# The second products of a feed-forward layer: 576 output columns as 384 and 192 instead of 288 and 288

## The chip, the core and the metric

The kernel runs on one core of a Trainium2 chip. The metric is device time in microseconds, the median of three runs. The engines are named as in the profile: PE (TensorE, products), PEld (its weight loads), DVE (VectorE), ACT (ScalarE), POOL (GpSimd), SP (SyncE, here mostly a queue that issues DMAs).

## The reference, cut to what matters

```python
def reference(A_u, A_A_re, ..., B_x, B_w1, B_w2):
    x = A_u                                   # 1 x 2048 x 576
    xn = _layernorm(x, axis=-1)
    return x + _A_ref(xn, ...) + _B_ref(xn, B_w1, B_w2)

def _B_ref(x, w1, w2):
    h = jnp.einsum("bsd,df->bsf", x, w1)      # 576 -> 4608
    h = _silu(h)
    return jnp.einsum("bsf,fd->bsd", h, w2)   # 4608 -> 576

def _A_ref(u, A_re, A_im, B_re, B_im, C_re, C_im, log_dt, Dskip):
    ...
    P = jnp.exp(logdA[:, :, None] * l[None, None, :])
    K = jnp.einsum("dn,dnl,dn->dl", Cc, P, dB).real   # a kernel of 2048 taps per channel
    ...                                               # FFT convolution of u with K
    return y + u * Dskip
```

The input x is normalised and goes two ways: through a long convolution whose kernel K is generated from a state-space model (128 states for each of 576 channels), and through a feed-forward layer with SiLU. Both results are added to x. All of it is in float32.

## The kernel before

**The feed-forward layer.** The 2048 rows are two halves of two blocks of 512 rows; a block is four row tiles of 128 (`j` is the row tile, 0 to 15). The 4608 hidden columns are nine chunks of `FT = 4` tiles of 128. Every pair of half, chunk and block is one entry of `blocks`, 36 in all. Each float32 operand is split into a high part, rounded to the format that PE multiplies in one pass (`F32R`), and a low part, the rest; a product of two such operands is three products: high by high, high by low, low by high. So `split_w1` and `split_w2` make `h1, l1` and `h2, l2` (ACT copies the high part, DVE subtracts for the low one), and `up` makes `gh, gl`.

`up(blk, t)` is a first product: 14 products of 512 columns into an accumulator `ph`, then SiLU and the copy to `gh` on ACT (L339, L340) and the subtraction to `gl` on DVE (L342). `down(blk, jj)` is the second product of one row tile with the four hidden tiles of the chunk: for each half of the 576 output columns (`HD = 288`) one accumulator `po`, 4 tiles by three products of 288 columns (L357), and an add of `po` to the row tile's sum `acc[j]` on DVE (L361). All accumulators `po` come from `ps2`, which has three buffers. The products of `up` use `ps1`, with two; everything else uses `pss`, with three.

**The order.** For each block eight steps are issued: `u0` of the next block, `d0` to `d3` of this one, `u1`, `u2`, `u3` of the next. The loads and splits of the next chunk's weights are hung behind steps. `weave` runs these 2 x 9 x 2 x 8 = 288 steps, and after each lets the generator `side()` go on to the share of the steps that it has asked for. `side()` does in turn: the normalisation and the transposes, the preparation of the parameters, the generation of K (`kgen`, between `marks[0]` and `marks[1]`; with it `spread`, the first transform of u), the spectral products (`spectral`, between `marks[1]` and `marks[2]`), and `tail`, which adds the convolution to the row tiles at the times `tail_at`. `kgen` works mostly on DVE (L637 to L676) with small products on PE (L696, L711); `spectral` uses all three engines (L826 is its products) and ends in `yo`, written to `d2`; `add_conv` reads it back as `ys` and multiplies once more (`py`, L847).

The order within an engine's queue is not this order: a scheduler places the instructions by a model of their times, priority going by the order of issue. `tc.high_priority()` lifts instructions (the adds of `po` and the SiLU group among them), and `behind(ins)` puts instructions after a given one on its engine. On the chip every engine then works through its own fixed queue.

**The end.** Row tiles 14 and 15 are stored last; row tile 15 in two halves of 288 columns (`store`, L184), each in four DMAs by two queues. The last chunk's weights for tiles 2 and 3 go into the pool `yp`, which opens when the spectral stage's pool `kl` has closed (L269, L304).

Of the kernel before, what the change touches and what calls it, by code (L numbers as in the profile page):

```python
# [11 lines left out]
F32 = mybir.dt.float32  # L12
F32R = mybir.dt.float32r
# [6 lines left out]
P = 128  # L20
L = 2048
D = 576
# [2 lines left out]
NJ = 16  # L25
NKT = 4
HD = D // 2
NFT = FF // P
MAGIC = 12582912.0
TWO_PI = float(np.nextafter(np.float32(2 * math.pi), np.float32(0)))  # L30
# [13 lines left out]
def kernel(  # L44
# [21 lines left out]
    nc = tc.nc  # L66
    FT = 4
    NCH = NFT // FT

# [4 lines left out]
    def quarters(v, engines):  # L74

        for q in range(4):
            yield slice(32 * q, 32 * q + 32), v[q // 2, q % 2], engines[q % len(engines)]
# [28 lines left out]
    wp = ctx.enter_context(tc.tile_pool(name="wp", bufs=2))  # L106
    gp = ctx.enter_context(tc.tile_pool(name="gp", bufs=6))
    ps1 = ctx.enter_context(tc.tile_pool(name="ps1", bufs=2, space=PSUM))
    ps2 = ctx.enter_context(tc.tile_pool(name="ps2", bufs=3, space=PSUM))
    pss = ctx.enter_context(tc.tile_pool(name="pss", bufs=3, space=PSUM))  # L110

    acc = {}
# [27 lines left out]
    pins = {}  # L140

    def behind(ins):
        return tc.issue_after(ins) if ins is not None else nullcontext()

    def spread(up):
# [3 lines left out]
        for j in range(NJ):  # L149
            src = up.tile([P, D], F32, tag="xr", name="xr")  # L150
            nc.sync.dma_start(src, dxn[:, j])
            for m in range(2):
# [5 lines left out]
                for h in range(2):  # L158
                    hs = slice(h * HD, (h + 1) * HD)
                    pu = pss.tile([P, 512], F32, tag="pss", name="pu")  # L160
                    nc.tensor.matmul(pu[:, :HD], s1[:, 0, :], sp[:, hs], start=True, stop=False)  # L161
                    nc.tensor.matmul(pu[:, :HD], s1[:, 1, :], sp[:, hs], start=False, stop=True)  # L162
                    nc.scalar.copy(u1[:, hs], pu[:, :HD])
                nc.gpsimd.dma_start(
# [3 lines left out]
    def load_x(j, pool, tag, engines):  # L168

        t = pool.tile([P, 2, D], F32, tag=tag, name=f"{tag}{j}")  # L170
        for i in range(2 if j == 0 else 1):
            for ps, v, eng in quarters(xv, engines):
                if j:
                    eng.dma_start(t[ps], v[:, j:j + 2])
                else:
                    eng.dma_start(t[ps, i], v[:, i])
        pairs[j] = t
        return t[:, 0, :], t[:, 1, :]

    def store(t, j, engines):  # L180

        for hs in (slice(0, HD), slice(HD, D)) if j == NJ - 1 else (slice(0, D),):
            for ps, v, eng in quarters(ov, engines):
                eng.dma_start(v[:, j:j + 2] if len(t.shape) > 2 else v[:, j, hs], t[ps] if len(t.shape) > 2 else t[ps, hs])  # L184

    def norm(p0, js, xs):
# [4 lines left out]
        for i in range(n):  # L191
            for h in range(2):
                nc.vector.bn_stats(out=st[:, i, h, :], in_=xs[i][:, h * HD:(h + 1) * HD])
            nc.vector.bn_aggr(out=mv[:, i, :], in_=st[:, i, :, :])
# [62 lines left out]
    def ffn():  # L257
        w2v = w2.rearrange("(t p) d -> p t d", p=P)
        blocks = [(half, c, b) for half in range(2) for c in range(NCH) for b in range(2)]
        W1, W2, G = {}, {}, {}  # L260
# [47 lines left out]
        def split_w2(half, c, t):  # L308
            first = half == 0 and c == 0
            r2 = R2.pop((half, c, t))  # L310
            h2 = wp.tile([P, D], F32R, tag="w2h", name="w2h", bufs=FT + 1)
            l2 = wp.tile([P, D], F32R, tag="w2l", name="w2l", bufs=FT + 1)
            with behind(pins["xt_s"] if first else pins["gh"]):
                pins["w2h"] = nc.scalar.copy(h2, r2).ins  # L314
            with behind(pins["w1l"] if first else None):
                pins["w2l"] = nc.vector.tensor_sub(l2, r2, h2).ins
            if first and t == 0:
                pins["w2l0"] = pins["w2l"]
            W2[half, c, t] = h2, l2

        def up(blk, t, a=0, e=512, after=None):

# [21 lines left out]
        def down(blk, jj):  # L344
            half, c, b = blk
            j = 8 * half + 4 * b + jj
            js = slice(jj * P, (jj + 1) * P)
            if half == 1 and c == NCH - 1:
                if jj % 2 == 0:
                    add_conv(j, (acc[j], acc[j + 1]))  # L350
            for h in range(2):
                hs = slice(h * HD, (h + 1) * HD)
                po = ps2.tile([P, 512], F32, tag="ps2", name="po")
                n = 0
                for t in range(FT):
                    for g, w in ((0, 0), (0, 1), (1, 0)):
                        pins["pe"] = nc.tensor.matmul(po[:, :HD], G[blk, t][g][:, js], W2[half, c, t][w][:, hs],  # L357
                                                      start=n == 0, stop=n == 3 * FT - 1).ins
                        n += 1
                with tc.high_priority():  # L360
                    nc.vector.tensor_add(acc[j][:, hs], po[:, :HD], acc[j][:, hs])  # L361
            if half == 0 and c == NCH - 1:
                rows = slice(j * P, (j + 1) * P)
                nc.sync.dma_start(dr0[rows, :], acc[j])
                if j % 2:
                    acc[7 + j], acc[8 + j] = load_x(7 + j, accp, "acc", (nc.sync,))
# [42 lines left out]
        for i, blk in enumerate(blocks):  # L409
            half, c, b = blk  # L410
# [451 lines left out]

    def side():
        nonlocal s4, kl, yp, pa, tail_at
        marks = (0.13, 0.597, 0.823)
        tail_at = (0.91, 0.934, 0.967, 0.0072)
        with tc.tile_pool(name="kf", bufs=1) as kfp:
            for n in ("f", "phi"):
                kf[n] = kfp.tile([P, D], F32, name=n + "T")
            with tc.tile_pool(name="par", bufs=1) as par:  # L870
                with tc.tile_pool(name="pa", bufs=4) as pa:

                    zero = pa.tile([P, 512], BF16, name="zero", bufs=1)
                    nc.vector.memset(zero, 0.0)
                    pz = ps1.tile([P, 512], F32, tag="ps1", name="pz")

                    def idle(n):
                        for _ in range(n):
                            nc.tensor.matmul(pz, zero[:, :P], zero, start=True, stop=True)

                    idle(12)
                    p01, p23 = phase0(pa, (0, 1), idle), phase0(pa, (2, 3))
                    next(p01)
                    yield 0
                    next(p23)
                    yield 0
                    next(p01)
                    yield 0
                    next(p23)
                    yield 0  # L890
                    for js in ((4, 5), (6, 7)):
                        with behind(pins["w2l0" if js[0] == 4 else "w2l"]):
                            for _ in phase0(pa, js):
                                pass
                    kf["dt"] = steps()
                    for n, ap in (("are", a_re), ("aim", a_im)):
                        kf[n] = par.tile([96, 6, NS], F32, tag=n, name=n)
                        nc.sync.dma_start(kf[n], ap.rearrange("(p t) n -> p t n", t=6))
                    yield 0
                with tc.tile_pool(name="nat", bufs=1) as nat, tc.tile_pool(name="pb", bufs=1) as pb:  # L900
                    nt = natural(nat, par)
                    def late(j):

                        xs = load_x(j, pb, "xj", (nc.sync,))
                        yield
                        with behind(pins["xn" if j == 8 else "gl"]):
                            normed(pb, (j, j + 1), xs)
                        yield

                    tiles = chain.from_iterable(late(j) for j in range(8, NJ, 2))  # L910
                    for at, todo in ((0.0, nt), (0.0, tiles), (0.004, tiles), (0.005, tiles), (gate_of(0), nt), (0.026, tiles), (0.028, tiles), (0.036, tiles), (0.038, tiles), (gate_of(1), nt), (0.06, tiles), (gate_of(2), nt), (0.09, nt)):
                        yield at
                        with behind(pins["gl"] if at else pins["xt7"] if todo is nt else None):
                            next(todo, None)
            with behind(pins["sd"]):
                nc.gpsimd.dma_start(f1, cf1)
            nc.sync.dma_start(vt, cv)
            with tc.tile_pool(name="up", bufs=1) as up:
                sp = spread(up)
                for n, at in enumerate(kgen()):  # L920
                    if n > 1:
                        next(sp, None)
                    yield marks[0] + at * (marks[1] - marks[0])
                for _ in sp:
                    pass
        s4p = ctx.enter_context(tc.tile_pool(name="s4p", bufs=1))
        s4 = s4p.tile([P, 32], F32, name="s4")
        nc.gpsimd.dma_start(s4, cs4)

        with tc.tile_pool(name="kl", bufs=2) as kl:  # L930
            for at in spectral():
                yield marks[1] + (at - 1) * (marks[2] - marks[1])
        yp = ctx.enter_context(tc.tile_pool(name="yp", bufs=3))
        yield from tail()
# [88 lines left out]
```

## Time and profile before

| | |
|---|---|
| median of 3 runs | 1110.36 us (1110.23 to 1110.42) |
| the profiled execution, first to last instruction | 1108.2 us |
| mean granted clock of PE | 1.000 |
| PE, PEld, DVE, ACT, POOL busy | 99%, 90%, 83%, 64%, 7% |
| products of L357 | 3 groups x 1152 |
| HBM read and written | 102.53 MB and 44.61 MB |

The profiled execution is one run of the program. Its own time is the span of 1108.2 us and what lies around it, about 2.2 us by the median of the runs. Groups are rows of line, engine, operation, output and inputs, shape and count; then busy time in us and the mean of one in ns; then idle time of the engine just before them and what ended it. A row of the chain or of a timeline begins with its start and its length in us. In a windows row, each engine's busy time in the stretch is followed by its count of instructions in brackets.

### The profile page before, as it was taken

To read this page: it belongs to the slowest core of one execution; us is meant where nothing else is said; L and a number is where in the kernel's file an instruction comes from. 1 tells how busy PE (TensorE), PEld (TensorE's weight loads), DVE (VectorE), ACT (ScalarE), POOL (GpSimd) and SP (SyncE) were. 2 spreads that over 40 slices of the span, in tenths; PEclk is the share of its full clock that TensorE was granted. 3 is DMA by queue.
4 is the path that set the end of the run, shared out by engine and by line. 5 is a ranking of instruction groups with operands and counts; after the bars stand their busy time and mean duration, and the time that the engine had idled before them with its cause. 6 is when DMAs were issued, how large, how long until landed. Compare 5 with 4: busy or idle time off the path is not lost.

```text
span 1108.2 us, 22917 instructions
## 1 busy us (share of the span) xinstructions
PE 1102.2 (99%) x9167; PEld 997.5 (90%) x9167; DVE 916.6 (83%) x1543; ACT 706.9 (64%) x1222; POOL 72.1 (7%) x129
## 2 busy tenths in 40 slices
PE   9999999999999999999999999999999999999998
PEld 7989998899998899899999989999999999999887
DVE  7799899999999999999999737787778778784433
ACT  4564466676677676677867536877777878774210
POOL 1100000000000000011000000000000000000111
PEclk9999999999999999999999999999999999999999
DMA  9745512525252525264744173554544455434983
GB/s 270 190 123 160 152 50 61 120 73 131 77 121 83 116 72 118 77 174 154 206 122 103 45 179 109 162 167 123 156 145 152 138 149 170 129 107 127 241 224 87
DMA packets 175755, 148.56 MB, mean 134 GB/s; under 512 B 111088, under 2 KB 142592, under 8 KB 175520
## 3 DMA queue, kind: packets, MB, share of 16 engines
q1 hardware_dynamic: 165328, 112.63, 38.7%
q0 software_dynamic: 9568, 33.62, 9.6%
q8 instruction: 72, 1.18, 0.5%
q10 hardware_dynamic: 752, 0.85, 0.3%
q14 instruction: 35, 0.29, 0.1%
HBM read 102.53 MB, written 44.61 MB: 133 GB/s over the span
## 4 chain that ended last, share of the span: by engine, by line
PE 98%; DMA 1%; DVE 1%; SPq 0%; issue 0%; DVEq 0%
PE po L357 42%; PE ph L331 35%; PE kp L696 3%; PE ph L332 3%; PE ph L333 3%; PE pu L826 2%; PE pb L826 2%; PE pk L826 2%; PE z L711 2%; PE pu L161 1%; PE py L847 1%; DMA acc<-in_A_u_dram 1%; PE pu L162 1%; PE pt L124 0%; DVE w1l L295 0%; PE ptk L490 0%
## 5 line engine op out<-in xcount | busy, mean ns | idle before, releaser
L357 PE MATMUL po<-w2l,gh 128*128 128x288 f32 x1152 | 338.5, 295 | 0.0
L357 PE MATMUL po<-w2h,gl 128*128 128x288 f32 x1152 | 336.4, 295 | 0.0
L357 PE MATMUL po<-w2h,gh 128*128 128x288 f32 x1152 | 336.1, 295 | 0.0
L357 PEld LDWEIGHTS po<-w2h,gh 128*128 128x128 f32 x1152 | 215.2, 188 | 7.7 <-issue 2.8
L357 PEld LDWEIGHTS po<-w2l,gh 128*128 128x128 f32 x1152 | 215.9, 188 | 5.1 <-issue 0.5
L357 PEld LDWEIGHTS po<-w2h,gl 128*128 128x128 f32 x1152 | 215.4, 188 | 0.9
L339 ACT ACTIVATE gf<-ph 128x512 f32<-128x512 f32 (+1 forms) x148 | 86.4, 584 | 143.8 <-PE ph L333 134.8
L331 PE MATMUL ph<-xh,w1l 128*128 128x512 f32 (+1 forms) x592 | 161.3, 385 | 0.0
L331 PE MATMUL ph<-xh,w1h 128*128 128x512 f32 (+1 forms) x592 | 161.3, 387 | 0.0
L331 PE MATMUL ph<-xl,w1h 128*128 128x512 f32 (+1 forms) x592 | 161.1, 385 | 0.0
L361 DVE TENSOR_TENSOR acc<-po,acc 128x288 f32<-128x288 f32 x288 | 126.2, 451 | 37.0 <-PE po L357 35.6
L342 DVE TENSOR_TENSOR gl<-gf,gh 128x512 fp32r<-128x512 f32 (+1 forms) x148 | 99.0, 672 | 64.6 <-ACT gh L340 63.8
L331 PEld LDWEIGHTS ph<-xh,w1l 128*128 128x128 f32 x592 | 108.0, 188 | 20.0
L331 PEld LDWEIGHTS ph<-xl,w1h 128*128 128x128 f32 x592 | 107.9, 188 | 19.8
L331 PEld LDWEIGHTS ph<-xh,w1h 128*128 128x128 f32 x592 | 104.5, 188 | 16.7 <-ACT x L133 0.5
L340 ACT CAST gh<-gf 128x512 fp32r<-128x512 f32 (+1 forms) x148 | 89.5, 608 | 9.5 <-PE po L357 6.6
L653 ACT ACTIVATE c<-th,magic 128x1040 f32<-128x1040 f32 x36 | 42.1, 1168 | 37.9 <-DVE C L676 28.0
L655 ACT ACTIVATE c<-th 128x1040 f32<-128x1040 f32 x36 | 38.7, 1075 | 33.6 <-DVE th L654 33.6
L314 ACT CAST w2h<-w2r 128x576 fp32r<-128x576 f32 x72 | 47.0, 671 | 17.7 <-PE po L357 14.9
L295 DVE TENSOR_TENSOR w1l<-w1r,w1h 128x640 fp32r<-128x640 f32 x72 | 56.9, 817 | 0.2
L332 PE MATMUL ph<-x,w1h 128*128 128x512 f32 (+1 forms) x148 | 57.0, 386 | 0.0
L333 PE MATMUL ph<-x,w1l 128*128 128x512 f32 (+1 forms) x148 | 56.9, 385 | 0.0
(185 smaller groups left out, 1828.8 us busy)
## 6 DMA issues: line engine op xcount, KB each, us to landing
w2r<-in_B_w_dram SPq DMA_DIRECT2D x72, 288.0 KB, 3.8
w1r<-in_B_w_dram SPq DMA_DIRECT2D x35, 512.0 KB, 3.8
d1u<-u POOLq DMA_DIRECT2D x32, 288.0 KB, 2.5
d1k<-stage SPq DMA_DIRECT2D x18, 512.0 KB, 6.8
ur<-d1u SPq DMA_DIRECT2D x32, 288.0 KB, 3.7
kr<-d1k SPq DMA_DIRECT2D x32, 288.0 KB, 2.9
d<-yo POOLq DMA_DIRECT2D x32, 288.0 KB, 4.0
ys<-d SPq DMA_DIRECT2D x32, 288.0 KB, 11.8
```

The costliest lines, as they stand in the source:

```text
L295: pins["w1l"] = nc.vector.tensor_sub(l1, src, h1).ins
L314: pins["w2h"] = nc.scalar.copy(h2, r2).ins
L331: nc.tensor.matmul(ph, w[:, kt, :], v[:, kt, a:e], start=n + kt == 0, stop=False)
L332: nc.tensor.matmul(ph, h1[:, 4, :], x4[:, a:e], start=False, stop=False)
L333: pins["pe"] = nc.tensor.matmul(ph, l1[:, 4, :], x4[:, a:e], start=False, stop=True).ins
L339: nc.scalar.activation(gf, ph, AF.Silu)
L340: pins["gh"] = nc.scalar.copy(gh, gf).ins
L342: pins["gl"] = nc.vector.tensor_sub(gl, gf, gh).ins
L357: pins["pe"] = nc.tensor.matmul(po[:, :HD], G[blk, t][g][:, js], W2[half, c, t][w][:, hs], start=n == 0, stop=n == 3 * FT - 1).ins
L361: nc.vector.tensor_add(acc[j][:, hs], po[:, :HD], acc[j][:, hs])
L653: nc.scalar.activation(c65, th, AF.Identity, bias=magic)
L826: nc.tensor.matmul(dst, st, mv[:, hs], start=n == 0, stop=n == 3 * len(terms) - 1)
```

## The change

The 576 output columns of a second product are divided as 384 (`DA`) and 192 (`DB`). High and low parts of a tile of w2 lie side by side in one SBUF tile `hl` of 128 x 2 x 576. For each hidden tile there are five products instead of six: `gh` by the 384 of the high part, `gh` by the 192 of both parts in one product of 384 columns (into `pb_`, high and low in separate columns), `gh` by the 384 of the low part, `gl` by the 192 of the high part, `gl` by the 384 of the high part. The accumulators `pa_` and `pb_` of a row tile are filled side by side. In the last hidden tile the product with both parts comes after the one of `gl`. Three adds follow: the two column groups of `pb_`, 192 each, then `pa_`, 384. The marks of `side()` move: generation ends at 0.613 of the steps instead of 0.597, the spectral stage at 0.836 instead of 0.823.

```diff
+DA = 384
+DB = D - DA
...
-            h2 = wp.tile([P, D], F32R, tag="w2h", name="w2h", bufs=FT + 1)
-            l2 = wp.tile([P, D], F32R, tag="w2l", name="w2l", bufs=FT + 1)
+            hl = wp.tile([P, 2, D], F32R, tag="w2s", name="w2s", bufs=FT + 1)
+            h2, l2 = hl[:, 0], hl[:, 1]
...
-            W2[half, c, t] = h2, l2
+            W2[half, c, t] = hl
...
-            for h in range(2):
-                hs = slice(h * HD, (h + 1) * HD)
-                po = ps2.tile([P, 512], F32, tag="ps2", name="po")
-                n = 0
-                for t in range(FT):
-                    for g, w in ((0, 0), (0, 1), (1, 0)):
-                        pins["pe"] = nc.tensor.matmul(po[:, :HD], G[blk, t][g][:, js], W2[half, c, t][w][:, hs],
-                                                      start=n == 0, stop=n == 3 * FT - 1).ins
-                        n += 1
+            pa_, pb_ = (ps2.tile([P, 512], F32, tag="ps2", name="po") for _ in range(2))
+            for t in range(FT):
+                (gh, gl), w = (g[:, js] for g in G[blk, t]), W2[half, c, t]
+                first, last = t == 0, t == FT - 1
+                nc.tensor.matmul(pa_[:, :DA], gh, w[:, 0, :DA], start=first, stop=False)
+                both = pb_[:, :2 * DB].rearrange("p (s d) -> p s d", s=2)
+                if not last:
+                    nc.tensor.matmul(both, gh, w[:, :, DA:], start=first, stop=False)
+                nc.tensor.matmul(pa_[:, :DA], gh, w[:, 1, :DA], start=False, stop=False)
+                nc.tensor.matmul(pb_[:, :DB], gl, w[:, 0, DA:], start=False, stop=False)
+                if last:
+                    nc.tensor.matmul(both, gh, w[:, :, DA:], start=False, stop=True)
+                pins["pe"] = nc.tensor.matmul(pa_[:, :DA], gl, w[:, 0, :DA], start=False, stop=last).ins
+            for hs, po in ((slice(DA, D), pb_[:, :DB]), (slice(DA, D), pb_[:, DB:2 * DB]), (slice(0, DA), pa_[:, :DA])):
                 with tc.high_priority():
-                    nc.vector.tensor_add(acc[j][:, hs], po[:, :HD], acc[j][:, hs])
+                    nc.vector.tensor_add(acc[j][:, hs], po, acc[j][:, hs])
...
-        marks = (0.13, 0.597, 0.823)
+        marks = (0.13, 0.613, 0.836)
```

## The prediction

> **What bounds the kernel now.** I read the page first: busy shares, then the chain, then the groups.
>
> ```profile
> span 1108.2 us, 22917 instructions
> PE 1102.2 (99%) x9167; PEld 997.5 (90%) x9167; DVE 916.6 (83%) x1543; ACT 706.9 (64%) x1222; POOL 72.1 (7%) x129
> ...
> PE 98%; DMA 1%; DVE 1%; SPq 0%; issue 0%; DVEq 0%
> ...
> L357 PE MATMUL po<-w2l,gh 128*128 128x288 f32 x1152 | 338.5, 295 | 0.0
> L357 PE MATMUL po<-w2h,gl 128*128 128x288 f32 x1152 | 336.4, 295 | 0.0
> L357 PE MATMUL po<-w2h,gh 128*128 128x288 f32 x1152 | 336.1, 295 | 0.0
> ...
> L361 DVE TENSOR_TENSOR acc<-po,acc 128x288 f32<-128x288 f32 x288 | 126.2, 451 | 37.0 <-PE po L357 35.6
> ```
>
> PE works all the time, and 98% of the chain that ended last is PE. The waits of PE confirm it; these are all of them, and both lie at the start:
>
> ```profile
> PE pz L879 <- DVE zero L874: 1.3, 1, 1.3
> PE pt L124 <- DVE xn L202: 0.4, 2, 0.2
> ```
>
> So the time is the sum of what each product costs PE, plus some 6 us at the two ends. The change rewrites 3 x 1152 = 3456 products of L357, in 576 passes of six (36 weight tiles by 16 row tiles). A product's duration (295 ns) overlaps its neighbours'; what counts is the distance from one start to the next. The chain view gives it, since it merges uninterrupted stretches of a line:
>
> ```profile
> 20.58 1.92 PE ph L331 x16
> 419.70 4.78 PE po L357 x36
> 424.48 0.69 PE ph L331 x3
> 1022.55 2.72 PE ph L331 x12
> ```
>
> The first row holds 256-column products (the first block runs in halves): 120 ns each. The second holds 288 columns: 132.8 ns. The last holds 512 columns: 226.7 ns. The line through the last two is 0.419 ns per column with 12 ns left over at zero columns, and it gives 119.4 ns for 256, where 120 was seen. So a product costs about 12 ns beside its columns, down to 256 columns.
>
> **What the change does to PE.** A pass keeps its 1728 columns (6 x 288 before; 4 x 384 + 192 after) and loses one product. On the line a 384-column product costs 132.8 + 96 x 0.419 = 173.0 ns, which lies between two rows and is safe. The 192-column product lies below every row of this kind, and here the loading of weights matters:
>
> ```profile
> L357 PEld LDWEIGHTS po<-w2h,gh 128*128 128x128 f32 x1152 | 215.2, 188 | 7.7 <-issue 2.8 <-DVE acc L361 0.4
> L696 PEld LDWEIGHTS kp<-S 128*32 128x32 f32 x1152 | 32.4, 110 | 0.0
> ```
>
> ```profile
> 197.32 0.19 PEld L357 LDWEIGHTS po<-w2l,gh 128*128 128x128 f32 x1
> 197.43 0.19 PEld L357 LDWEIGHTS po<-w2h,gl 128*128 128x128 f32 x1
> 197.57 0.19 PEld L357 LDWEIGHTS po<-w2h,gh 128*128 128x128 f32 x1
> ...
> 410.04 0.19 PEld L357 LDWEIGHTS po<-w2h,gl 128*128 128x128 f32 x1
> ```
>
> ```profile
> 410.04 0.29 PE L357 MATMUL po<-w2l,gh 128*128 128x288 f32 x1
> ```
>
> Every product has a load of 128 columns. In the stream a load starts with the product before its own (410.04 in both views), not sooner, though a 512-column product leaves the loader idle: one load ahead is all there is. How long does it hold the loader? At 197.32, after the small products of generation, no product runs over the first load, and the next load follows 0.11 us later; then they fall back to the product's pace (0.14, 0.13). The durations agree: 96 columns more make 78 ns more, 0.81 ns per column, so 128 columns take 104 ns. A product of 192 columns streams in 80 ns, so its successor's weights come last: I take 110 ns for it. Ends of the bound: 92.6 ns (the line, if loads hide), 132.8 ns (the 288-column row, since a narrower product should not cost more).
>
> In this place the Trainium skill speaks against the change: TensorE: Matmul & The Clock Gate, section LDWEIGHTS (loading the stationary operand), makes a load last its columns over 1.2 ns, an estimate of 107 ns for 128 columns. The trace agrees with its 104 and 110 ns. By that figure alone the sum below would be 1.7 us smaller.
>
> The sum per pass: removed 6 x 132.8 = 796.8 ns; added 4 x 173.0 + 110 = 802.0 ns; +5.2 ns, by 576 passes **+3.0 us**. The ends are -12.2 ns (-7.0 us) and +28.0 ns (+16.1 us). The product over high and low weights together reads its columns in two runs; no row shows such an operand, and I take nothing for it, between nothing and what the upper end holds.
>
> **DVE.** The two adds of 288 columns per row tile become three of 192, 192 and 384, because high and low weights' parts of the 192 come in separate columns.
>
> ```profile
> 64.59 1.17 DVE L361 TENSOR_TENSOR acc<-po,acc 128x288 f32<-128x288 f32 x3
> 404.28 1.24 DVE L637 TENSOR_TENSOR th<-vt,fT 128x1040 f32<-128x1040 f32 x1
> 408.51 1.28 DVE L639 TENSOR_TENSOR th<-th,phiT 128x512 f32<-128x512 f32 x2
> 410.45 0.75 DVE L660 TENSOR_TENSOR C<-pw,wb 128x256 f32<-128x256 f32 x2
> ```
>
> Back to back, an add costs (1.17 - 0.45) / 2 = 0.36 us; by the same subtraction 512 columns cost 0.60 us (1.28 less 0.68 for one) and 256 cost 0.33 (0.75 less 0.42). That is 1.04 ns per column, so 192 cost 0.27 and 384 cost 0.47: 1.01 us in place of 0.72, **+0.29 us** for each of 144 accumulations into a row tile, 42 us of DVE in all. Is it hidden? The windows over generation:
>
> ```profile
> 140.00:660.00 520.00, 520.00 (x5350) 469.01 (x5349) 485.84 (x729) 351.64 (x528) 23.52 (x42) 1.00 0.41 108
> 250.00:400.00 150.00, 150.00 (x1645) 134.92 (x1644) 147.91 (x220) 106.14 (x159) 5.93 (x11) 1.00 0.40 104
> ...
> 140.00:660.00 520.00, 60.66 (x140) 1.00 0.41 108
> ```
>
> The third figure is DVE: 485.8 of 520 us, and 147.9 of 150 in the tightest stretch. The last row is L361 alone: 140 adds, so 70 accumulations, +20 us. The marks move from 0.597 to 0.613, which gives generation 1.6% more of the steps, about 17.7 us. The two nearly cancel, and DVE stays just below full: hidden on average. Without the cover it would cost a part of those 20 us. The adds and the gl splits have high priority, so generation gives way first and PE is still fed. Splitting w2 into one tile instead of two issues the same copies, subtractions and loads: nothing. The steps of generation and of the spectral stage that move take their DMAs with them, on SP's queue (base tables, staged results, parts of u and k) and on POOL's. They pass up to 4.6 of the 288 steps' loads of w1 and w2 there.
>
> ```profile
> w2r<-in_B_w_dram SPq DMA_DIRECT2D x72, 288.0 KB, 3.8
> w1r<-in_B_w_dram SPq DMA_DIRECT2D x35, 512.0 KB, 3.8
> ```
>
> Such a load lands 3.8 us after its issue and is asked for a chunk ahead, two blocks of about 1108 / 36 = 31 us, which hides it: nothing; without that cover 3.8 us each.
>
> **The end.** The last stores wait for the last add:
>
> ```profile
> 1103.62 0.29 PE L357 MATMUL po<-w2h,gl 128*128 128x288 f32 x1
> ...
> 1103.95 0.46 DVE L361 TENSOR_TENSOR acc<-po,acc 128x288 f32<-128x288 f32 x1 [1.14 <-PE po L357]
> ...
> 1104.43 0.79 SPq L184 DMA_DIRECT2D out_dram<-acc  x2
> ```
>
> Today the first 288 columns of row tile 15 are added and stored while the second half is still multiplied. After the change the 384-column part is added last, and both halves of the store touch it: 4 issues per queue after the last add instead of 2, at 0.79 / 2 = 0.4 us, and an add 0.1 us longer. Together **+0.9 us**, all on the path.
>
> **Total.** The profiled execution is 1108.2 us; the median of the runs is 1110.4, so 2.2 us lie around the span. 1110.4 + 3.0 + 0.9, and 1 us that I allow for waits of PE that do not exist today (their price is below): **1115 us**.
>
> **Rivals.**
> *Faster: the load hides after all.* If weights of the product after next may be loaded early, the 192 costs 92.6 ns, and 1110.4 - 7.0 + 0.9 = 1104 us. For it: the line is straight down to 256. Against: the restart at 197.32, and the load that never starts before the preceding product. The deciding point is the 192's distance: under 105 ns the PE sum falls. The Trainium skill has a rule of that kind (TensorE: Matmul & The Clock Gate, section Back-to-back issue gap: columns over 2.4 plus 2.5 ns); its estimate for 192 columns is 82.5 ns, but by it 512 columns would take 215.8 ns, where the trace shows 226.7.
>
> *Slower: accumulators run short.* There are three ps2 buffers. The chain row of 36 products is three accumulations of twelve, after which PE turns to ph. Now a row tile opens two at once and both end together. When the next row tile starts, its 384 part has the third buffer, 12 x 173 = 2.08 us of work; then the narrow part needs a buffer back, some 0.33 us of product tail (the last product's start at 1103.62 to the add at 1103.95, above) and two adds of 0.27. That is 0.87 us with DVE free, covered. With two generation operations of 1.24 us ahead on DVE's queue it is 3.35 us, 1.27 uncovered unless a ph is ready. In generation 70 accumulations have 52 boundaries inside a block; a third of them uncovered costs 17 x 1.27 = 22 us: 1110.4 + 3.9 + 22 = 1136 us. For it: DVE is full there. Against: PE's order is planned, and it has ph products to put in.
>
> *Slower: the last chunk comes late.* The load of the last weights waits for the spectral stage's buffers:
>
> ```profile
> 1009.41 0.52 PE pb L826 x4
> 1096.20 1.15 PE py L847 x32
> ...
> 1013.35 0.38 SPq L278 DMA_DIRECT2D w1r<-in_B_w_dram  x1
> ```
>
> Work that needs it or the spectral output: six ph steps of 14 x 0.227 us, two blocks of 96 x 0.1328 and eight py pieces of 1.15 us, 54 us; it can begin as late as 1104 - 54 = 1050. The load and split take until about 1022, so 28 us are spare. The marks shift generation by some 18 us; if DVE's load holds the spectral stage back by over 10 us more, the excess shows at the end: 5 us of it gives 1119 us.
>
> **Chances.** The forecast 0.45 (own range 1110 to 1121); loads hidden 0.18; accumulators short 0.25; late chunk 0.12. About 0.2% is what a measurement of this kernel can tell from no change: 2.2 us, so 1108.1 to 1112.6. Faster: the hidden load and a little of mixtures, 0.2. Within: the lower part of the forecast, 0.15. Slower: 0.65. Range 1104 to 1137: from the hidden load to the short accumulators.
>
> **What would show it.** Right: 2880 products of that line, the 384s at 173 ns, the step from the 192 to its successor near 110 ns, PE still above 98% of the span, four store issues behind the last add. Wrong: a step near 93 ns (then faster), PE waits on L361's successors of more than a few us, or PE idle between 1030 and 1060 us.

## The result and the profile after

The changed kernel takes 1162.28 us (median of 6 runs, 1157.17 to 1166.54) against 1110.39 us: 1.0463 of the time before, 95% interval 1.0447 to 1.0479. The prediction had 1115 us and at most 1137. It is slower, as forecast, but by 52 us in place of 5. The profile below is of the slowest of the six runs, the one of 1166.54 us.

The page of the kernel after, in the parts shown of before:

```profile
span 1164.8 us, 21987 instructions
PE 1128.2 (97%) x8591; PEld 1012.4 (87%) x8591; DVE 954.5 (82%) x1687; ACT 705.5 (61%) x1222; POOL 71.2 (6%) x129
...
PE 73%; DVE 13%; DMA 4%; ACT 3%; issue 3%; SPq 2%; POOL 0%; ACTq 0%; DVEq 0%; POOLq 0%
...
L368 DVE TENSOR_TENSOR acc<-po,acc 128x192 f32<-128x192 f32 (+1 forms) x432 | 168.9, 417 | 46.1 <-PE po L364 31.7
```

PE lost its hold on the chain: 98% before, 73% now. Its time not busy rose from 6.0 us (1108.2 - 1102.2) to 36.6 (1164.8 - 1128.2), and its busy time rose by 26.0. DVE is busy 37.9 us longer, and yet its share fell; the adds alone went from 126.2 us to 168.9, 42.7 us more, where 42 were predicted. Of PE's waits there had been two rows in all; these are the four longest now:

```profile
PE ph L333 <- ACT w1h L295: 10.5, 2, 9.3
PE ph L333 <- ACT gf L341: 7.6, 4, 3.0
PE py L854 <- DMA ys<-d: 4.0, 1, 4.0
PE po L357 <- ACT w2s L316: 3.2, 2, 2.5
```

They sit in three places: early, while the parameters are prepared; in generation (the 2.5 us for `w2s`, at 522 us); and at the last chunk. The timeline shows one early wait (from 99.8 us on) and the two large ones at the last chunk:

```profile
99.42 0.36 PE L365 MATMUL po<-w2s,gl 128*128 128x384 f32 x1
101.68 1.44 PE L333 MATMUL ph<-xh,w1h 128*128 128x512 f32 x4 [1.90 <-ACT gf L341]
102.92 1.91 PE L333 MATMUL ph<-xl,w1h 128*128 128x512 f32 x4
...
1082.26 2.08 PE L333 MATMUL ph<-xh,w1h 128*128 128x512 f32 x4 [9.26 <-ACT w1h L295]
...
1094.39 1.23 PE L854 MATMUL py<-ys,s 64*32 64x288 f32 x32 [4.00 <-DMA ys<-d]
```

The queues around the last chunk say why. Before:

```profile
L778 ACT COPY yo<-pb x64: 385/399/408, 690.0 to 1010.0; 128x288 f32<-128x288 f32 x64
SPq L278 <- DMA d<-yo: 10.1, 2, 6.8
```

After (the first row gives the first and the last start of the copies that end the spectral stage; the second what SP's queue waited for; the others are timelines of SP and ACT):

```profile
L785 ACT COPY yo<-pb x64: 388/400/410, 740.9 to 1073.3; 128x288 f32<-128x288 f32 x64
SPq L280 <- DMA d<-yo: 45.2, 1, 45.2
1076.75 0.38 SPq L280 DMA_DIRECT2D w1r<-in_B_w_dram  x1
1081.48 1.35 ACT L295 CAST w1h<-w1r 128x640 fp32r<-128x640 f32 x2 [7.77 <-DMA w1r<-in_B_w_dram]
```

The spectral stage ends 63 us later (1073.3 against 1010.0). SP's queue stands 45 us at the load of the last weights, ACT waits 7.8 us and PE 9.3 us for them, and the convolution's data come 4 us too late as well. Of the 63 us, 51 are there when these copies begin (740.9 against 690.0); the spectral stage itself then takes 12 us longer.

In this run every wait of PE of 1.9 us or more costs twice. The windows (PE, PEld, DVE, ACT, POOL busy, then the granted clock):

```profile
60.00:110.00 50.00, 45.07 (x204) 38.82 (x203) 41.34 (x73) 27.60 (x34) 1.67 (x2) 0.90 0.54 140
1070.00:1100.00 30.00, 16.63 (x93) 13.49 (x92) 5.89 (x10) 5.04 (x9) 3.06 (x6) 0.77 0.82 198
```

The clock was 1.000 before and is 0.986 over the whole span now: some 31 us at half clock, or 16 us of full speed lost, in pieces that begin in or just behind the waits. The four products at 102.92 are such a piece, 1.91 us where four of 512 columns usually show 1.07.

The products themselves kept to the prediction, by their medians. Timelines of PE and PEld of one pass:

```profile
302.26 0.33 PE L361 MATMUL po<-w2s,gh 128*128 128x384 f32 x1
302.44 0.25 PE L362 MATMUL po<-w2s,gl 128*128 128x192 f32 x1
302.53 0.36 PE L365 MATMUL po<-w2s,gl 128*128 128x384 f32 x1
302.72 0.34 PE L357 MATMUL po<-w2s,gh 128*128 128x384 f32 x1
...
302.44 0.19 PEld L365 LDWEIGHTS po<-w2s,gl 128*128 128x128 f32 x1
302.55 0.19 PEld L357 LDWEIGHTS po<-w2s,gh 128*128 128x128 f32 x1
```

The record of the product after the 192 opens 88 ns behind it, which looks as if the load were hidden. But that product lasts 197 ns to the next start instead of 174, and the following load starts at 302.55, not at 302.53: it had waited 23 ns for its weights. Medians over the trace: 88 + 197 - 174 = 111 ns for the 192, where 110 was taken. If the load were hidden, the two together would take 92.6 + 173 = 266 ns by the line of the prediction; they take 285.

### The profile page after: what moved, and what is told of

Read it like the earlier page. It is cut to its first block, busy times and chain, and to the rows that moved or that the text cites. A ratio compares the mean times of both kernels' runs of the same rounds, so it can differ in the third digit from the quotient of the medians.

```text
span 1164.8 us, 21987 instructions
## 1 busy us (share of the span) xinstructions
PE 1128.2 (97%) x8591; PEld 1012.4 (87%) x8591; DVE 954.5 (82%) x1687; ACT 705.5 (61%) x1222; POOL 71.2 (6%) x129
## 4 chain that ended last, share of the span: by engine, by line
PE 73%; DVE 13%; DMA 4%; ACT 3%; issue 3%; SPq 2%; POOL 0%; ACTq 0%; DVEq 0%; POOLq 0%
PE ph L333 25%; PE po L357 7%; PE po L365 7%; PE po L361 7%; PE po L360 6%; PE po L362 4%; PE pk L833 2%; PE pu L833 2%; PE kp L703 2%; PE ph L335 2%; PE ph L334 2%; PE po L364 2%; PE pb L833 2%; DVE acc L368 2%; DMA w2r<-in_B_w_dram 1%
## 5 line engine op out<-in xcount | busy, mean ns | idle before, releaser
L368 DVE TENSOR_TENSOR acc<-po,acc 128x192 f32<-128x192 f32 (+1 forms) x432 | 168.9, 417 | 46.1 <-PE po L364 31.7
L357 PE MATMUL po<-w2s,gh 128*128 128x384 f32 x576 | 196.6, 343 | 4.1 <-ACT w2s L316 3.2
L365 PE MATMUL po<-w2s,gl 128*128 128x384 f32 x576 | 197.3, 344 | 0.0
L361 PE MATMUL po<-w2s,gh 128*128 128x384 f32 x576 | 194.2, 338 | 0.0
L333 PE MATMUL ph<-xh,w1h 128*128 128x512 f32 (+1 forms) x592 | 166.5, 393 | 18.2 <-ACT w1h L295 10.5
L333 PE MATMUL ph<-xl,w1h 128*128 128x512 f32 (+1 forms) x592 | 165.8, 392 | 0.0
L360 PE MATMUL po<-w2s,gh 128*128 128x384 f32 x432 | 139.0, 351 | 0.9 <-DVE acc L368 0.9
L333 PEld LDWEIGHTS ph<-xh,w1h 128*128 128x128 f32 x592 | 108.4, 190 | 36.0 <-ACT w1h L295 11.2
L362 PE MATMUL po<-w2s,gl 128*128 128x192 f32 x576 | 136.8, 255 | 0.9 <-DVE gl L344 0.9
L357 PEld LDWEIGHTS po<-w2s,gh 128*128 128x128 f32 x576 | 109.5, 190 | 10.9 <-ACT w2s L316 3.8
L362 PEld LDWEIGHTS po<-w2s,gl 128*128 128x128 f32 x576 | 108.6, 190 | 4.5 <-DVE gl L344 1.3
L361 PEld LDWEIGHTS po<-w2s,gh 128*128 128x128 f32 x576 | 109.2, 190 | 2.1 <-DVE w2s L318 0.2
L365 PEld LDWEIGHTS po<-w2s,gl 128*128 128x128 f32 x576 | 109.0, 189 | 0.5
L360 PEld LDWEIGHTS po<-w2s,gh 128*128 128x128 f32 x432 | 81.9, 190 | 6.0 <-DVE acc L368 1.6
L316 ACT CAST w2s<-w2r 128x576 fp32r<-128x576 f32 x72 | 47.5, 672 | 32.6 <-DMA w2r<-in_B_w_dram 25.0
```

The costliest lines, as they stand in the source:

```text
L333: nc.tensor.matmul(ph, w[:, kt, :], v[:, kt, a:e], start=n + kt == 0, stop=False)
L357: nc.tensor.matmul(pa_[:, :DA], gh, w[:, 0, :DA], start=first, stop=False)
L360: nc.tensor.matmul(both, gh, w[:, :, DA:], start=first, stop=False)
L361: nc.tensor.matmul(pa_[:, :DA], gh, w[:, 1, :DA], start=False, stop=False)
L362: nc.tensor.matmul(pb_[:, :DB], gl, w[:, 0, DA:], start=False, stop=False)
L365: pins["pe"] = nc.tensor.matmul(pa_[:, :DA], gl, w[:, 0, :DA], start=False, stop=last).ins
```

## The experiments

Times are medians, each against the kernel before on the same chip (1110.1 to 1110.5 us).

**Marks and order.** Four kernels separate three theories of the loss: the moved marks (M), the opening of two accumulators at once (S) and the third add (A). Later texts add P: the products' new sizes and their order.

The changed kernel with the old marks:

```diff
-        marks = (0.13, 0.613, 0.836)
+        marks = (0.13, 0.597, 0.823)
```

> The changed kernel with the marks of before (0.597 and 0.823). Three theories of the 52 us. S, two accumulators opened at once: the stalls before generation stay, since no mark lies there, and so does their delay: 1145 to 1165 us. M, generation and the spectral stage put later, so that the last chunk's weights come late: the 20 us around the last chunk (a wait of 9.3, one of 4.0 and 14 us at half clock) go, 1135 to 1145 us, or less if the early stalls too come of the order. A, DVE overfull by the third add: generation at the old pace is worse, over 1165 us.

1146.16 us, 1.0324 (1.0308 to 1.0339): the marks cost the changed kernel 16 us. The time lies in the range of S and just above that of M; the early waits stay, and the last chunk's wait falls to 4.6 us. So M is right about a third of the loss.

The kernel before with the new marks, the same line the other way:

> The kernel before with the marks of the change (0.613 and 0.836), all products and adds as before. S and A: no loss, 1109 to 1114 us, the spectral stage ending some 18 us later than 1010 us. M: 1125 us or more, with PE waiting for the last chunk's weights near 1030 to 1060 us.

1119.80 us, 1.0082 (1.0065 to 1.0099): the marks alone cost 10 us, more than S and A allow and less than M asked. The copies end later, and PE waits:

```profile
L778 ACT COPY yo<-pb x64: 385/399/419, 710.3 to 1028.7; 128x288 f32<-128x288 f32 x64
PE py L847 <- DMA ys<-d: 4.3, 2, 3.0
```

It is not the weights that are late first but `ys`, the convolution's data, with the spectral stage 19 us later. From the last part of the wait of 3.0 us on the clock was halved for 6.8 us, some 3 us of full speed more.

The changed kernel, all products of the 384 columns first, then those of the 192:

```diff
-            pa_, pb_ = (ps2.tile(...) for _ in range(2))
...
+            pa_ = ps2.tile([P, 512], F32, tag="ps2", name="po")
+            for t in range(FT):
+                ...   # gh, high; gh, low; gl, high: 384 columns
+            add(slice(0, DA), pa_[:, :DA])
+            pb_ = ps2.tile([P, 512], F32, tag="ps2", name="po")
+            ...       # the eight products of pb_, then its two adds
```

> The changed kernel with its two accumulators opened one after the other: all twelve products of the 384 columns, then the eight of the 192; products, adds and marks as in the change, only their order differs. S: PE's waits go; 5 us for the products and 1 us at the end remain, 1114 to 1120 us. M: the late last chunk stays, 1135 us or more. A: DVE has the same three adds, 1150 us or more.

1152.57 us, 1.0380 (1.0365 to 1.0396). That is 10 us less than the change, but S expected 1114 to 1120; the waits stayed, the last chunk's above all, and the time lies in the ranges of M and A:

```profile
PE ph L333 <- ACT w1h L295: 11.0, 3, 9.7
PE ph L333 <- ACT gf L341: 6.9, 6, 2.0
```

The kernel before with its two accumulators filled side by side:

```diff
-            for h in range(2):
-                po = ps2.tile(...)
+            pos = [ps2.tile(...) for _ in range(2)]
+            for t in range(FT):
+                for n, (g, w) in enumerate(((0, 0), (0, 1), (1, 0))):
+                    for h in range(2):
+                        ...   # the product of half h into pos[h]
```

> The kernel before with both 288-column accumulators of a row tile opened at once and filled in turn; six products, two adds and the marks of before. S: PE waits appear before and in generation, 1130 us or more. M and A: 1109 to 1113 us, nothing that they name has changed.

1113.39 us, 1.0028 (1.0017 to 1.0038): 3 us, with 1.5 us more of waits than before. S falls for these products. For those of the change the sequential order is tried once more, with the old marks:

> The sequential order of e3 with the marks of before and all three adds; against 1146 us (side by side, same marks). So far the three known pieces, from 1110 us: products 8 to 10 us, the third add 12 to 16, the marks 10 to 16. If opening two accumulators at once costs what e3 showed (10 us), this is 1134 to 1138 us; if e3's 10 us were only the late end shrinking, 1144 us or more.

1149.98 us, 1.0361 (1.0344 to 1.0378), 4 us more than side by side. So the 10 us of e3 come only with the late marks.

**The third add.** Taken away, with the old marks:

```diff
-            for hs, po in ((slice(DA, D), pb_[:, :DB]), (slice(DA, D), pb_[:, DB:2 * DB]), (slice(0, DA), pa_[:, :DA])):
+            for hs, po in ((slice(DA, D), pb_[:, :DB]), (slice(0, DA), pa_[:, :DA])):
```

> The changed kernel with the marks of before and without the add of the low weights' part of the 192 columns, so that part is left out of the sum: DVE does two adds per row tile (192 and 384) instead of three; PE's products are those of the change. To be compared with 1146 us for the same marks and three adds. A, the third add's 0.27 us of DVE is what starves PE: its 17 us of waits and 7 us of half clock nearly go, and the products' 8 to 10 us stay, 1118 to 1126 us. P, the order that the products' new sizes give to PE and ACT: little changes, 1138 us or more.

1134.27 us, 1.0217 (1.0200 to 1.0234): 12 us less than with three adds, between the ranges of A and P. Added to the kernel before:

```diff
                     nc.vector.tensor_add(acc[j][:, hs], po[:, :HD], acc[j][:, hs])
+                    if h:
+                        nc.vector.tensor_add(scr, po[:, :224], acc[j][:, :224])
```

> The kernel before with a third add on DVE after each row tile's second one: 224 columns of the second accumulator and of acc into a scratch tile that nobody reads, about 0.30 us, as much as the change adds. Products and marks are those of before. A: PE waits appear before generation and at the last chunk, 1125 to 1140 us. P: 1110 to 1113 us.

1126.59 us, 1.0147 (1.0132 to 1.0162): 16 us from 0.3 us of DVE per accumulation, on a kernel whose DVE was 83% busy, as A expected. Its waits and the end of its spectral stage:

```profile
PE po L358 <- DVE acc L362: 4.4, 1, 4.4
PE py L850 <- DMA ys<-d: 2.5, 1, 2.5
L781 ACT COPY yo<-pb x64: 389/400/413, 719.9 to 1036.9; 128x288 f32<-128x288 f32 x64
```

The add delays the spectral stage by 27 us, though the marks are the old ones: DVE is nearly full in generation, and the last z product starts at 678 us instead of 643. The windows of this run over generation:

```profile
140.00:660.00 520.00, 518.59 (x5216) 467.24 (x5215) 506.65 (x803) 350.52 (x528) 22.09 (x40) 1.00 0.39 105
```

DVE is busy 97% here, 93% before. But PE loses only 1.4 us in these 520; its longer waits lie in front of generation and behind the spectral stage. The longest, in front, is a wait for an accumulator, and DVE was not full then: its queue stood at a load of x, with the adds behind it.

```profile
113.05 1.54 DVE L194 BATCH_NORM_STATS2 st<-xj 128x6 f32<-128x288 f32 x4 [4.61 <-DMA xj<-in_A_u_dram]
116.73 0.40 PE L358 MATMUL po<-w2h,gh 128*128 128x288 f32 x1 [4.38 <-DVE acc L362]
```

SP's queue issued these loads at 108.1 us, where before they stood at 93.7; why the add moves them so far is not shown. PE's waits in this run are 10 us longer than before, and the half clock behind the two long ones takes 3.4 us of full speed: 13 of the 16 us. Both together, the third add and the new marks on the kernel before:

> The kernel before with the third add of e6 and the marks of the change; products as before. If the pieces add, 1126.6 + 9.7 = 1136 us. If the marks make room for the add, as the change's description has it, 1120 to 1127 us.

1141.30 us, 1.0279 (1.0264 to 1.0294). The pieces add, and a little more (16 + 10 = 26; 31 measured). The marks make no room for the add:

```profile
PE ph L332 <- ACT w1h L294: 10.5, 2, 9.6
PE po L358 <- DVE acc L362: 4.8, 3, 4.4
PE py L850 <- DMA ys<-d: 2.3, 1, 2.3
L781 ACT COPY yo<-pb x64: 390/400/406, 719.5 to 1050.7; 128x288 f32<-128x288 f32 x64
```

Three fifths of the loss stand here, in a kernel with the products of before, and the wait of 9.6 us for the last chunk's weights is like the 9.3 us of the changed kernel.

**The end.** The last chunk's weights loaded like every other chunk's:

```diff
-            r1 = (pa if first and t else yp if last and t else wp).tile(...)
+            r1 = (pa if first and t else wp).tile(...)
...
-            if new == (1, NCH - 1):
+            if False:
```

> The changed kernel with the marks of before, and the last chunk's weights loaded into the same buffers and at the same steps as every other chunk's, not into the pool that opens when the spectral stage has ended. To be compared with 1146 us. If the end of the spectral stage holds PE back only through these weights, the wait of 4.6 us near 1062 and 7 us at half clock (3.4 us of loss) go: 1136 to 1140 us. If the convolution's own data (ys) or the row tiles are late too, 1144 us or more.

1155.83 us, 1.0403 (1.0386 to 1.0420), 10 us worse than the kernel that it alters. The wait for the first weights went, but those of the second product now queued on SP behind the convolution's loads, and PE stood 11.8 us for them by way of ACT. This kernel has a new delay of its own, so it doesn't say whether the weights alone hold PE back. The marks one step earlier say more:

> The changed kernel with marks one more step the other way, 0.581 and 0.81. If the late last chunk is what the marks cost, the wait at the last chunk (4.6 us and 7 us at half clock at 0.597) goes and no more: 1136 to 1140 us. If DVE is overfull at that pace, generation runs late all the same and the time stays at 1146 us or rises.

1141.82 us, 1.0288 (1.0273 to 1.0303). No wait of PE is left behind 410 us, but ahead of it stand 13.5 us of waits more than in the kernel before, and the gain against the old marks is 4 us: between the two expectations. The late last chunk went, as the first had it, and the early waits stayed.

**What is left.** With two adds and the old marks 24 us stay, whether the accumulators are opened together (e5) or in turn:

```diff
             add(slice(DA, D), pb_[:, :DB])
-            add(slice(DA, D), pb_[:, DB:2 * DB])
```

> The same without the add of the low weights' part of the 192 columns, which is left out of the sum: sequential, marks of before, two adds. What is left against before is the products. Additive pieces: 1119 to 1123 us (products 9 us, nothing else). If the sizes disturb the order beyond their own time, 1128 us or more.

1133.54 us, 1.0210 (1.0195 to 1.0225), in the second range: the order in which the two accumulators are filled is not what is left. The products' own part is the mean distance from a product's start to the next start on PE, where no wait and no half clock lies between. In e1 it is 181.8 ns for 384 columns and 91.5 for 192, so 4 x 181.8 + 91.5 = 819 ns per pass, against 6 x 133.8 = 803 before: 16 ns, 9 us. The other 15 us:

> The changed kernel with two adds (the low weights' part of the 192 columns left out) and the marks 0.581 and 0.81; against 1134.3 us with the marks of before. If what is left there beside 9 us of products is the late end of the spectral stage (a wait of 3.9 us for ys and 3.4 us lost to half clock), this is 1125 to 1129 us and no PE wait stands behind 1000 us. If the order of the wide products costs elsewhere, 1132 us or more.

1132.75 us, 1.0203 (1.0180 to 1.0225). The wait at the end falls from 3.9 us to 0.8, and the half clock behind it is gone (mean clock 0.999 against 0.997), yet only 1.5 us is won, and these four runs spread over 4.3 us. That is the second range, if barely. What waits here, all of it ahead of 600 us:

```profile
PE ph L333 <- ACT gf L341: 3.9, 2, 2.0
PE ph L333 <- ACT w1h L295: 1.7, 1, 1.7
PE po L357 <- ACT w2s L316: 1.5, 2, 1.0
```

PE is not busy for 16.2 us here, 10.2 more than before. With the products' 9 us that is most of the 21.6 us by which the span is longer.

More work on PE alone, in the kernel before:

```diff
-                        ... W2[half, c, t][w][:, hs], ...
+                        ... W2[half, c, t][w][:, 280 * h:280 * h + 296], ...
```

> The kernel before with second products of 296 columns instead of 288 (8 columns of each half are multiplied twice and not added twice): PE's own work rises by 3456 x 8 x 0.42 ns = 11.6 us, about what the change's products add, with the sizes and the number of products and all adds as before. If more PE work alone makes the spectral stage end late and the end wait, 1126 us or more; if it only adds itself, 1120 to 1124 us, and the period of the spectral stage stays near 10.3 us.

1128.61 us, 1.0162 (1.0144 to 1.0180). The products cost 137.8 instead of 133.8 ns, 13.8 us, and 18.3 us came: again waits in the early stage, 3.6 us, and none at the end. The time is in the first range, but not for its reason: the spectral stage ends 16 us later (1025.8) and PE does not wait there.

```profile
PE ph L331 <- ACT w1h L293: 2.4, 1, 2.4
PE ph L331 <- ACT gf L339: 1.3, 1, 1.3
```

So longer products by themselves can bring early waits. Why the wide products bring more of them is open: the sizes, their order, and the joint tile `hl`, which no run tries by itself, stand together in every kernel that has them.

**Other widths.** 320 and 256, so that no product is under 256 columns:

```diff
-DA = 384
+DA = 320
```

> The changed kernel with the marks of before and the columns divided as 320 and 256, so that no product is narrower than 256 columns and the one with both parts is 512. By the line of the products a pass costs 3 x 146 + 227 + 120 = 785 ns, 30 ns less than the 816 measured for the change: PE's own work falls by 17 us. DVE's adds cost 1.07 us per row tile instead of 1.01. A: the waits stay or grow, 1128 to 1140 us. P: the waits depend on the sizes and can go, 1105 to 1125 us.

1152.78 us, 1.0377 (1.0361 to 1.0392), against 1146 for 384 and 192, above both ranges. The products are cheaper (148.4 ns for 320 columns, 236.5 for 512 and 119.5 for 256, a pass of 801 against 819, and 803 before), but PE is not busy for 33.6 us, 27.6 more than before, and the clock falls to 0.988: the waits decide, not the products. No version beat the kernel before.

## Why the prediction was right and wrong

**The products: right in kind, too small in size.** The medians are 111 ns for the 192 against 110 and 174 for a 384 against 173; the load of the next weights sets the 192's, as the restart at 197.32 had said. The rival in which the load hides is refuted. The sum had 802.0 ns for a pass against 796.8. The medians make it 4 x 174 + 111 = 807 against 6 x 133 = 798, but the means, which count, 819 against 803: 9 us, not 3.0. So this term was a third of its size; what lifts the means above the medians isn't shown. Here the Trainium skill (TensorE: Matmul & The Clock Gate, section LDWEIGHTS) agrees with the trace: the estimate of 107 ns per load that its rule gives stands beside the 111.

**DVE: the step that failed.** The 0.29 us per accumulation was right (42.7 us more of adds). "Hidden on average" was not. The sum took generation's windows, 485.8 of 520 us, added 20 us, gave back 17.7 by the marks, and called the rest cover. e6 shows what the add costs: 16 us on the kernel before. That PE is still fed in generation was right (518.6 of 520 us in e6); the cost falls ahead of it and behind it. Ahead, DVE was no less full, and the prediction did not look there:

```profile
60.00:120.00 60.00, 60.00 (x360) 54.49 (x359) 57.82 (x100) 35.13 (x46) 3.27 (x3) 1.00 0.54 137
```

DVE is busy 57.8 of 60 us in this stretch of the kernel before. In e6 it is busy only 51.1 us there, since its queue stands at a late load, and PE waits 4.4 us. In the changed kernel the add shows in other rows: without it (e5 against e1) PE's idle time is 6 us shorter. Behind, the late generation (35 us) makes the spectral stage 27 us late, and PE waits 2.5 us for `ys`. The marks, booked as the counterweight, are a second charge at that end: 10 us alone (e2), 15 us with the add (e12), 16 us in the changed kernel (e1).

**The late last chunk: the right mechanism, priced and weighed too low.** It had 0.12 and 5 us. A second step that failed is "28 us are spare": it followed the weights alone. The convolution's data come through the same end, and e2 shows PE waiting for them when the stage is only 19 us late. And the shift was taken as the marks' 18 us and perhaps 10 more; it was 63.

**Accumulators running short: not at its price.** It had 0.25 and 22 us. In the changed kernel PE waits 1.8 us for an add to give an accumulator back:

```profile
PE po L360 <- DVE acc L368: 0.9, 2, 0.6
PE po L357 <- DVE acc L368: 0.9, 1, 0.9
```

Filling them in turn won 10 us with the new marks (e3) and lost 4 with the old ones (e9), and filling them side by side in the kernel before cost 3 us (e4). What the rival saw rightly is that PE can run out of other work. Most of the early waits of the changed kernel are for ACT, to split weights or to read with SiLU one of the two accumulators of `up`; only in e6 and e12, where DVE's queue stood, is the longest early wait one for a `po`.

**Half clock: missing.** "1 us of waits" had no price for what follows a wait. The clock's 0.986 is 16 us of full speed; part of it fell into the waits themselves and cost nothing.

**The sum as measured.** Third add 16 us, marks 15 us on top of it (e12: 31); what the products bring 21 us more, 9 of it their own time. The other way down, 16 us for the marks, 12 for the add, 24 left: the same 52. These are differences between runs, so each sum comes to 52 by itself; beside the products' own 9 us the last piece holds 12 or 15 us, mostly waits of PE and the half clock behind them, and why these come is open. The four issues behind the last add, 0.9 us predicted, show as 5.4 us from the start of the last product to the end against 4.6.

## What to carry to other kernels

An engine that is nearly full in a stage on which later stages hang (DVE: 93% here, 97% with the add) can be on the path, even when another engine is busy 100% beside it: don't call its extra work hidden by an average, and follow what ends later. Look at every stage that gets some of that work, not only at the one that gets most: in a fixed queue one late load holds up all that stands behind it. Look for everything that a late stage releases, not only for the nearest consumer; the tightest of them sets the slack. Judge a product that is narrower than its weight load takes by the distance to the second start behind it, since the delay shows on the next product's record.

## What the runs showed of the hardware that was not expected

PE's clock falls to half behind short waits. In the changed kernel gaps of 1.9, 2.0, 2.6, 3.0, 4.0 and 9.3 us were followed by 3.4 us at half clock, or a multiple; a gap of 1.3 us was not. In e13 gaps of 1.9 and 2.0 us and in e14 one of 2.4 were not either, while in e8 two gaps of 0.9 and 1.4 us that end 1.8 us apart were. So about 2 us of idle can be enough, but needn't be. Each 3.4 us of work at half clock takes 1.7 us more than at full clock.
